# A PSUM bank lent to weight conversion, and the eighth attention unit in two-part operands

## The chip, the cores and the metric

The kernel runs on 1 core of one Trainium2 chip. The metric is the device time of one execution in microseconds. Before the change it is 1041.06 us, the median of 3 runs (1039.58 to 1042.63).

## The reference

Forget-gate attention, then two MLPs, all in float32 (the MLP weights arrive as float64):

```python
# q, k, v: 4 x 8 heads x 576 x 64; s: 4 x 8 x 576
cum = np.cumsum(np.maximum(s, 0.0), axis=-1)
scores = scale * q @ k^T + np.minimum(-(cum[..., :, None] - cum[..., None, :]), 0.0)   # causal
attn = np.exp(scores - rowmax); attn /= attn.sum(-1) + 1e-09
x = (attn @ v) as 2304 tokens x 512
r = np.maximum(x @ w_in, 0.0);  x = (s * (r * r) + b) @ w_out          # 512 -> 2048 -> 512
h = x @ w_in2;  out = (np.maximum(h, 0) + alpha * np.minimum(h, 0)) @ w_out2
```

## The kernel before

**Precision.** A product is made either with native float32 operands, which TensorE passes over twice (two records in the trace for one matmul), or with operands split into a high and a low fp32r part (`split`, L129): high x high, high x low, low x high. Attention's split form makes scores with two matmuls (L459, L460) where the native form has one (L457), and it splits the transposed probabilities into `ph` and `pl` instead of copying them to `pf` (L518 to L525).

**Attention.** A unit is one batch, one half of the tokens (`rng`: queries 0 to 319, or 320 to 575) and one pair of heads: 32 units. For each head, `scores` builds the bias in `probs` (VectorE L435, for the second head of a native unit ScalarE L431 with a sign flip), masks the diagonal on GpSimd (L439), adds TensorE's scores with a running extreme (L461), takes the exponential (L473), turns the sums round (L480, L481) and multiplies by them on GpSimd (L484). `values` transposes the probabilities (TensorE `pt`, L515), brings them to SBUF and multiplies by v (`av`, L531); the result goes into `xf`, the next layer's input. Units below `NATIVE` (L55, 8) use native float32, the others split operands. A split unit needs more: copies and differences of q and k (L393 to L401), the split of v into `vs` (L360 to L367), and the sum of two halves of `av` (L548, L549).

**Order.** Units 0 to 3 come first, with little beside them (0 to 61.6 us, "the head" here). Then layer 1 of the reference runs (called layer 0 in the code) in blocks of 256 tokens, `up` (L783) and `down` (L897) over 16 slices f of the 2048 hidden columns; units 4 to 7 are worked in beside block 0, the rest beside the later blocks. Block 1's input needs unit 7. The second MLP runs mostly in pairs of token blocks by Strassen's scheme: each pair of slices takes three banks a, b, c (L854), one of which (b) is read last by VectorE (L884). The instruction order on every engine is set by the framework's scheduler, which simulates a time line as it goes and gives pool buffers to whichever tile can have one; a change in any wait or buffer can reorder what follows.

**Weights.** Packet f holds slice f of both weight matrices. `fetch` loads 512 KB of raw pairs for each matrix on SyncE's queue, into whatever buffer the string `RAW` (L166) names: "raw", "xh1", "xl1", "xh0", "xl0", "res" or "vs". `convert` (L134) makes float32 of them in three steps over 128 x 512: ScalarE Prelu into `wt` (L140), VectorE shift of `wt` in place (L141), VectorE shift of the raw low word and OR with `wt` (L142); `split` then makes the high and low parts (L130 ScalarE, L131 VectorE for w_in and GpSimd for w_out). Packets 0 to 3 are asked for in the head, packets 4 to 15 during block 0, four slices ahead (`AHEAD`, L59).

**PSUM.** Eight banks of 128 x 512 float32: two for `acc0`, `acc1`, one for `hp`, one for `av`, and four with the tag "b", a pool from which scores, transposes and, in the later stages, `hp` and Strassen's a, b, c take any free one.

Of the kernel before, what the change touches and what calls it, by code (L numbers as in the profile page):

```python
# [8 lines left out]
F32 = mybir.dt.float32  # L9
F32R = mybir.dt.float32r  # L10
U32 = mybir.dt.uint32
BF16 = mybir.dt.bfloat16
AF = mybir.ActivationFunctionType
ALU = mybir.AluOpType
# [5 lines left out]
def tile_forget_attention__then__two_mlps(  # L20
# [20 lines left out]
    nc = tc.nc  # L41
    B, H, S, D = q.shape
    NT, DM = out.shape
    DFF = w_in1.shape[1] // 2
    P = 128
    NP = H // 2
    NCC = DM // P
    NF = DFF // P
    T = 256
# [2 lines left out]
    IB = [(0, 64)] + [(64 + 128 * n, 192 + 128 * n) for n in range(4)]  # L52
    R1 = IB[2][1]
    QK = S - R1 + S
    EARLY, NATIVE = NP, 2 * NP  # L55

    LAG, AHEAD, LEAD, PACE = (2, 3), 4, 4, 1.25  # L59
# [13 lines left out]
    ps = ctx.enter_context(tc.tile_pool(name="ps", bufs=2, space=PSUM))  # L73
# [24 lines left out]

    busy(16)

    def load_constants():
        nc.sync.dma_start(out=gate_s, in_=act_s.partition_broadcast(P))
        nc.sync.dma_start(out=gate_b, in_=act_b.partition_broadcast(P))
        nc.sync.dma_start(out=nalpha, in_=alpha.rearrange("(f p) -> p f", p=P))
        nc.vector.tensor_scalar(out=nalpha, in0=nalpha, scalar1=-1.0, scalar2=None, op0=ALU.mult)
        nc.vector.tensor_scalar(out=gate_s, in0=gate_s, scalar1=1.0 / W_SCALE, scalar2=None, op0=ALU.mult)
        nc.vector.tensor_scalar(out=gate_b, in0=gate_b, scalar1=1.0 / W_SCALE, scalar2=None, op0=ALU.mult)

    def sum_gates(first):

        nc.vector.tensor_scalar(out=gates, in0=gates, scalar1=0.0, scalar2=1.0 / SCALE, op0=ALU.max, op1=ALU.mult)
        ones = one.tile([B * H, S], F32, tag="vn", name="ones")
        nc.vector.memset(ones, 1.0)
        cum = two.tile([B * H, S], F32, tag="cum", name="cum")
        nc.vector.tensor_tensor_scan(out=cum, data0=ones, data1=gates, initial=0.0, op0=ALU.mult, op1=ALU.add)
        nc.scalar.dma_start(out=cum_d, in_=cum)
        for h, pool, tag in ((0, ps_h, "hp"), (1, ps, "av")):
            rows = pool.tile([P, 512], F32, tag=tag, name=f"rows{h}", bufs=1)[:, :R1]
            nc.tensor.matmul(
                rows, ident[: B * H, h : h + 1].to_broadcast([B * H, P]), cum[:, :R1], start=True, stop=True  # L120
            )
            first.cums.append(rows)
        tp = ps.tile([P, 5, B * H], F32, tag="b", bufs=4, name="tp")
        for r, (i0, i1) in enumerate(IB):
            nc.tensor.transpose(tp[: i1 - i0, r], cum[:, i0:i1], ident[: B * H, : B * H])
        nc.vector.tensor_copy(cumT[:64, 0], tp[:64, 0])
        nc.vector.tensor_copy(cumT[:, 1:], tp[:, 1:])
# [3 lines left out]
        lo_eng.tensor_tensor(out=lo, in0=src, in1=hi.bitcast(F32), op=ALU.subtract)  # L131


    def convert(raw, wt):  # L134

        low, high = raw[:, :, 0], raw[:, :, 1]

        nc.scalar.activation(wt.bitcast(F32), high.bitcast(F32), AF.Prelu, scale=REBASE, alpha=-(2.0**32))  # L140
        nc.vector.tensor_scalar(out=wt, in0=wt, scalar1=3, scalar2=None, op0=ALU.logical_shift_left)  # L141
        nc.vector.scalar_tensor_tensor(  # L142
            out=wt, in0=low, scalar=29, in1=wt, op0=ALU.logical_shift_right, op1=ALU.bitwise_or
        )

    def slot(n, dtype, name):
# [15 lines left out]
    PAIRS = {  # L162
        "r": [(two, "raw"), (two, "raw")], "x": [(one, "xh1"), (one, "xl1")], "y": [(one, "xh0"), (one, "xl0")],
        "v": [(one, "res"), (one, "vs")], "m": [(one, "res"), (two, "raw")], "n": [(two, "raw"), (one, "res")],
    }
    RAW = [pair for key in "rxyvrxvrxvrxvrmn" for pair in PAIRS[key]]  # L166
    SLOT, free = {}, list(range(NF))
    for f in range(len(SPARE), NF):
        at = int((f - len(SPARE)) * PACE)
# [46 lines left out]
    def load_packet(layer, f):  # L216
        wi, wo = fetch(layer, f)
        t = weight_tiles(f) if layer == 1 else []
        values_ = []
        for n, src in enumerate((wi, wo)):  # L220
            if layer == 1:
                pool, tag, cols = WT[(2 * f + n) % len(WT)]
                wt = pool.tile([P, cols], U32, tag=tag, name=f"wt{f}_{n}")[:, :512]
            elif (f, n) == (NF - 1, 1):
                wt = two.tile([P, 512], U32, tag="ph", name="last")
            else:
                wt = slot(WHOLE[f][n], U32, f"wt0_{f}_{n}")
            convert(src, wt)
            values_.append(wt.bitcast(F32))
        for n, wt in enumerate(values_):  # L230
            if layer == 0:
                t += [slot(m, F32R, f"w0_{f}_{len(t)}_{m}") for m in SPLIT[f][2 * n : 2 * n + 2]]
            split(t[2 * n], t[2 * n + 1], wt, nc.gpsimd if layer == 0 and n else nc.vector)
        return [x.rearrange("p (c n) -> p c n", c=NCC) for x in t[:2]] + t[2:]


    def sum_columns():

        ones = two.tile([P, T], F32, tag="r", name="ones")[:, :P]
        nc.gpsimd.memset(ones, 1.0)  # L240
        ones_r = two.tile([P, T], F32R, tag="r", name="ones_r")[:, :P]
        nc.scalar.copy(ones_r, ones)
        total = ps.tile([P, 512], F32, tag="b", name="colsum", bufs=4)
        for n in range(2 * NF):
            nc.tensor.matmul(total, ones_r, packet(0, n // 2)[2 + n % 2], start=(n == 0), stop=(n == 2 * NF - 1))
        colw = two.tile([P, 512], F32, tag="ph", name="colw")
        nc.scalar.copy(colw, total)
        turned = ps.tile([P, 512], F32, tag="b", name="colsum_t", bufs=4)
        for d in range(NCC):
            nc.tensor.transpose(turned[:, d * P : (d + 1) * P], colw[:, d * P : (d + 1) * P], ident)  # L250
        for d in range(NCC):
            nc.vector.tensor_scalar(
                out=bsum[:, d : d + 1], in0=turned[:, d * P : d * P + 1], scalar1=gate_b[:, 0:1], scalar2=None,
                op0=ALU.mult,
            )
# [22 lines left out]
    class Unit:  # L278
# [21 lines left out]
        def bank(self, tag, name):  # L300
            name = f"{name}_{self.tag}"
            self.n_banks += 1
            if self.n < EARLY and self.n_banks % 2:
                if tag == "tr":
                    return ps_h.tile([P, 512], F32, tag="hp", name=name)
                if tag == "av":
                    return acc_first
            if tag == "av":
                return ps.tile([P, 512], F32, tag="av", name=name, bufs=1)
            return ps.tile([P, 512], F32, tag="b", name=name, bufs=4)  # L310

    def qk_tiles(u, dtype, tag):

# [446 lines left out]
    def mlp_block(layer, t, x):  # L760
# [11 lines left out]
        def up(f):  # L772
            w = packet(layer, f)
            if layer == 0 and count == 1:
                hp = ps_h.tile([P, 512], F32, tag="hp", name=f"hp{layer}_{t}_{f}")
            else:
                hp = ps.tile([P, 512], F32, tag="b", name=f"hp{layer}_{t}_{f}", bufs=4)
            hs = hp[:, :TB]
            terms = ((w[0], xh), (w[0], xl), (w[1], xh))
            n = 0  # L780
# [65 lines left out]
        def up_first(f):  # L846

            name = f"{t}_{f}"
            (h1, l1), (h2, l2) = halves(f), halves(f + 1)
            left = {1: (h1[:, 0], l1[:, 0]), 2: (h1[:, 1], l1[:, 1]), 4: (h2[:, 1], l2[:, 1])}  # L850
            for n, k in ((5, 1), (6, 2), (7, 3), (3, 4)):
                both = sums[(k - 1) // 2][:, (k - 1) % 2]
                left[n] = both[:, : 2 * P], both[:, 2 * P :]
            a, b, c = (ps.tile([P, 512], F32, tag="b", name=f"p{z}_{name}", bufs=4)[:, :T] for z in range(3))  # L854
            t1, t5, u2 = temp("gh", f"t1_{name}", 3), temp("gl", f"t5_{name}", 3), temp("gh", f"u2_{name}", 3)
            multiply(a, 1, left[1], True)
            nc.scalar.copy(t1, a)
            multiply(b, 6, left[6], True)
            nc.vector.tensor_tensor(out=u2, in0=b, in1=t1, op=ALU.add)  # L859
            multiply(c, 5, left[5], True)  # L860
            nc.scalar.copy(t5, c)
            holder = []
            pair_state[f // 2] = left, (a, b, c), (t1, t5, u2), holder
            next_sums(f, (0, 1))
            return holder
# [121 lines left out]
    for n in range(len(BLOCKS) * NF):  # L987
        (layer, t), f = BLOCKS[n // NF], n % NF
        if f == 0:
            up, down, finish = mlp_block(layer, t, x)  # L990
            goal, x = reached(min(t + 1, NB - 1)) if layer == 0 else len(units), None
        late.append((down, finish, f, up(f)))
        if layer == 0 and t == 0 and f + AHEAD < NF:
            with tc.issue_after(relus[f - 1]) if f else nullcontext():
                packet(0, f + AHEAD)
            for g in range(f + AHEAD + 1, min(f + AHEAD + 3, NF)):
                fetch(0, g)
        if n == NF - 2:
            sum_columns()
        if len(late) > LAG[layer]:  # L1000
# [51 lines left out]
```

## Time and profile before

| What | Value |
|---|---|
| Time, median of 3 runs | 1041.06 us (1039.58 to 1042.63) |
| Profiled execution, whole | 1040.97 us |
| Its span (first to last work) | 1039.2 us |
| PE (TensorE matmul) busy | 1019.4 us, 98% |
| DVE (VectorE) / ACT (ScalarE) / POOL (GpSimd) busy | 66% / 65% / 44% |
| Granted TensorE clock, mean | 0.996 of full |

The page gives busy shares over the whole span. PE is the busiest by far, so time is gained where PE has less to do or waits less. The share does not tell at which places PE waits; those are read from stretches (windows) and time lines. In a time line the start of one matmul to the start of the next is what it costs, since matmuls are pipelined and their lengths overlap.

### The profile page before, as it was taken

What the parts mean: (1) busy time and instruction counts of PE and PEld (TensorE: products, weight loads), DVE (VectorE), ACT (ScalarE), POOL (GpSimd) and SP (SyncE); (2) the same over time, 40 slices, a digit from 0 to 9 for tenths busy, and PEclk for the clock granted to TensorE, in tenths of its full rate; (3) what the DMA queues carried; (4) which work ended last, traced back from release to release, by engine and by line L of the source; (5) the groups of instructions that cost most, each with busy time, mean ns of one, the idle gap of its engine ahead of it and who ended that gap; (6) DMA issues with size and microseconds to landing.
All of it is one profiled execution on the core that took longest, in us unless ns stands there. A gap on an engine that the chain in (4) does not pass through costs nothing. (4 is left out here: it accounts for less than half of the span.)

```text
span 1039.2 us, 20636 instructions
## 1 busy us (share of the span) xinstructions
PE 1019.4 (98%) x6952; PEld 925.8 (89%) x6952; DVE 681.3 (66%) x1605; ACT 672.4 (65%) x1669; POOL 457.6 (44%) x876
## 2 busy tenths in 40 slices
PE   9899999999999999999999999999999999999997
PEld 4568899999999999999999888888899999999996
DVE  6979865787676776677655865857665456455443
ACT  5877876777787877778776776645454455445433
POOL 5656775666677666777562000574611011001000
PEclk9999999999999999999999999999999999999999
DMA  7988433343232432334215762645644335334331
GB/s 167 255 211 239 132 68 70 71 93 79 40 92 64 102 72 52 79 68 91 66 35 173 240 192 74 207 147 170 196 163 142 103 112 172 103 99 136 104 104 46
DMA packets 197930, 125.45 MB, mean 121 GB/s; under 512 B 138496, under 2 KB 167936, under 8 KB 197824
## 3 DMA queue, kind: packets, MB, share of 16 engines
q1 hardware_dynamic: 193744, 123.56, 42.8%
q8 instruction: 55, 0.90, 0.4%
q10 hardware_dynamic: 4080, 0.57, 0.3%
q14 instruction: 51, 0.42, 0.1%
HBM read 106.19 MB, written 17.90 MB: 119 GB/s over the span
## 5 line engine op out<-in xcount | busy, mean ns | idle before, releaser
L783 PE MATMUL hp<-xh,w 128*128 128x256 f32 (+1 forms) x1024 | 229.0, 300 | 0.3 <-ACT r L802 0.3
L907 PE MATMUL acc<-w,ring 128*128 128x512 f32 x864 | 214.6, 392 | 1.1 <-DVE ring L131 0.7
L907 PEld LDWEIGHTS acc<-w,ring 128*128 128x128 f32 x864 | 155.8, 188 | 29.3 <-DVE ring L131 1.1
L783 PEld LDWEIGHTS hp<-xh,w 128*128 128x128 f32 x1024 | 171.4, 189 | 6.2 <-ACT r L802 0.5
L897 PE MATMUL acc<-gh,w 128*128 128x256 f32 x896 | 172.4, 286 | 0.5 <-ACT res L926 0.5
L783 PE MATMUL hp<-xl,w 128*128 128x256 f32 (+1 forms) x512 | 152.6, 298 | 0.0
L897 PEld LDWEIGHTS acc<-gh,w 128*128 128x128 f32 x896 | 136.0, 189 | 3.2 <-issue 1.6
L883 POOL TENSOR_TENSOR cc<-u,t 128x256 f32<-128x256 f32 x32 | 26.1, 817 | 235.5 <-DVE u L874 201.5
L897 PE MATMUL acc<-gl,w 128*128 128x256 f32 x448 | 118.7, 288 | 2.2 <-POOL gl L131 2.2
L484 POOL TENSOR_SCALAR probs<-probs,sm 64x64 f32<-64x64 f32 (+4 forms) x160 | 91.0, 581 | 60.5 <-DVE sm L481 49.9
L473 ACT ACTIVATE probs<-probs,nm 64x64 f32<-64x64 f32 (+4 forms) x160 | 90.0, 563 | 38.5 <-DVE nm L461 32.7
L131 POOL TENSOR_TENSOR gl<-r,gh 128x256 fp32r<-128x256 f32 x112 | 89.5, 799 | 48.6 <-ACT gh L130 42.1
L817 PE MATMUL p<-xs,sums 128*128 128x256 f32 x768 | 104.7, 282 | 0.4 <-DVE u L859 0.4
L783 PEld LDWEIGHTS hp<-xl,w 128*128 128x128 f32 x512 | 97.1, 190 | 3.3 <-issue 0.4
L817 PEld LDWEIGHTS p<-xs,sums 128*128 128x128 f32 x768 | 98.0, 189 | 2.1 <-DVE u L859 0.6
L461 DVE CUSTOM_DVE_ANT_0 probs<-sc,probs 128x320 f32<-128x320 f32 (+3 forms) x160 | 68.2, 427 | 41.2 <-PE sc L460 32.8
L817 PEld LDWEIGHTS p<-xs,w 128*128 128x128 f32 x576 | 79.0, 189 | 8.7 <-DVE u L874 2.0
L802 ACT ACTIVATE r<-hp 128x256 f32<-128x256 f32 (+1 forms) x144 | 58.0, 403 | 44.1 <-PE hp L783 33.2
L817 PE MATMUL p<-xs,w 128*128 128x256 f32 x576 | 82.3, 282 | 2.4 <-DVE u L874 1.5
L897 PEld LDWEIGHTS acc<-gl,w 128*128 128x128 f32 x448 | 80.1, 188 | 5.0 <-POOL gl L131 2.8
L828 DVE SCALAR_TENSOR_TENSOR ph<-pl,misc,ph 128x512 f32<-128x512 f32 x64 | 51.7, 807 | 42.4 <-ACT pl L844 42.4
L515 PE MATMUL pt<-ident,probs 128*128 128x128 f32 x480 | 74.3, 275 | 4.6 <-POOL probs L484 4.4
(149 smaller groups left out, 2116.8 us busy)
## 6 DMA issues: line engine op xcount, KB each, us to landing
sums<-sums_d SPq DMA_DIRECT2D x128, 256.0 KB, 2.7
wi<-in_moe_w_in_dram SPq DMA_DIRECT2D x32, 512.0 KB, 4.7
wo<-in_moe_w_out_dram SPq DMA_DIRECT2D x32, 512.0 KB, 4.8
cum<-cum_d SPq DMA_DIRECT2D x32, 288.0 KB, 3.7
sums_d<-w SPq DMA_DIRECT2D x64, 128.0 KB, 1.8
cum<-cum_d SPq DMA_DIRECT2D x30, 160.0 KB, 3.0
nat<-in_k_dram SPq DMA_DIRECT2D x64, 72.0 KB, 2.5
x_d<-res SPq DMA_DIRECT2D x18, 256.0 KB, 2.2
```

What stands on the lines that cost most here:

```text
L131: lo_eng.tensor_tensor(out=lo, in0=src, in1=hi.bitcast(F32), op=ALU.subtract)
L461: nc.vector.tensor_tensor_reduce(out=pt[:rows, j0:j1], in0=scr, in1=pt[:rows, j0:j1], scale=SCALE if flip else -SCALE, scalar=init, op0=AL ...
L473: nc.scalar.activation(pt[:rows, :n], pt[:rows, :n], AF.Exp, bias=nm[:rows, m : m + 1], scale=1.0 if flip else -1.0, accum_out=sm[:rows, m ...
L484: nc.gpsimd.tensor_scalar(out=probs[r][:rows, :n], in0=probs[r][:rows, :n], scalar1=sm[:rows, m : m + 1], scalar2=1.0, op0=ALU.mult, op1=A ...
L515: nc.tensor.transpose(tp[:, o : o + P], u.probs[h][r][:, k0 : k0 + P], ident)
L783: nc.tensor.matmul(hs, a[:, c], b[c], start=(n == 0), stop=(n == len(terms) * NCC - 1))
L802: relus.append(nc.scalar.activation(r, hs, AF.Relu, scale=1.0 / W_SCALE).ins)
L817: nc.tensor.matmul(bank, lhs[:, c * P : (c + 1) * P], rhs[:, c], start=(start and c == 0 and z == 0), stop=(c == 1 and z == 2), skip_group ...
L828: nc.vector.scalar_tensor_tensor(out=r, in0=u, scalar=nalpha[:, f : f + 1], in1=r, op0=ALU.mult, op1=ALU.add).ins
L883: nc.gpsimd.tensor_tensor(out=cc[:, T:], in0=u3, in1=t5, op=ALU.add)
L897: nc.tensor.matmul(banks[d] if count == 2 else acc[d // 2][:, d % 2], a[:, d * P : (d + 1) * P], b, start=(f == 0 and (d % 2 == 0 or count ...
L907: nc.tensor.matmul(banks[m], a[:, m * P : (m + 1) * P], b, start=(f == 0 and b is woh and a is gh), stop=(f == NF - 1 and a is gl),)
```

## The change

Four things change:

- `NATIVE` goes from 8 to 7: unit 7 (batch 0, second half, head pair 3), worked in beside the end of block 0, uses split operands.
- The tag "b" with four buffers becomes four tags b0 to b3 with one buffer each, handed out in a fixed rotation in the order in which the program asks (`bank`).
- From the first `up` of block 0 until slice 12, the rotation runs over three banks, and the fourth takes the result of the shift in `convert`: 24 conversions (packets 4 to 15, both matrices) shift from SBUF into PSUM, and OR from PSUM and the raw word into `wt`.
- In `RAW`, packet 12's w_out goes to "raw" where it had "vs", because unit 7 now has `vs`.

```diff
-    EARLY, NATIVE = NP, 2 * NP
+    EARLY, NATIVE = NP, 7
...
+    turn, lent = [0], []
+    def bank(name, n=None):
+        if n is None:
+            turn[0] += 1
+            n = turn[0] % (3 if lent else 4)
+        return ps.tile([P, 512], F32, tag=f"b{n}", name=name, bufs=1)
...
-    def convert(raw, wt):
+    def convert(raw, wt, shifted):
...
-        nc.vector.tensor_scalar(out=wt, in0=wt, scalar1=3, scalar2=None, op0=ALU.logical_shift_left)
+        nc.vector.tensor_scalar(out=shifted, in0=wt, scalar1=3, scalar2=None, op0=ALU.logical_shift_left)
         nc.vector.scalar_tensor_tensor(
-            out=wt, in0=low, scalar=29, in1=wt, op0=ALU.logical_shift_right, op1=ALU.bitwise_or
+            out=wt, in0=low, scalar=29, in1=shifted, op0=ALU.logical_shift_right, op1=ALU.bitwise_or
         )
...
-    RAW = [pair for key in "rxyvrxvrxvrxvrmn" for pair in PAIRS[key]]
+    RAW = [pair for key in "rxyvrxvrxvrxmrmn" for pair in PAIRS[key]]
...
-            convert(src, wt)
+            convert(src, wt, bank(f"bits{f}_{n}", 3).bitcast(U32) if lent else wt)
...
-            return ps.tile([P, 512], F32, tag="b", name=name, bufs=4)
+            return bank(name)
...
-            a, b, c = (ps.tile([P, 512], F32, tag="b", name=f"p{z}_{name}", bufs=4)[:, :T] for z in range(3))
+            a, b, c = (bank(f"p{z}_{name}")[:, :T] for z in range(3))
...
+        if n == 0:
+            lent.append(3)
...
+        if n == NF - AHEAD:
+            lent.clear()
```

The scheduler's order changes from the head onward. Two places, with the lines of each kernel's own file (L141, L142, L131, L375, L435, L480, L481 of before are L147, L148, L140, L381, L441, L486, L487 of after).

VectorE in the head, around the end of unit 3's second head (`sm_3_0_1` holds its sums; `wt_4` is packet 4, `turned_0_1` and `probs_0_1_0` belong to unit 4). Before:

```order
L470 TENSOR_SCALAR nm_3_0_1_722<-nm_3_0_1_722 128x1
L141 TENSOR_SCALAR wt_4_0_901<-wt_4_0_901 128x512
L131 TENSOR_TENSOR xl_0_870<-xf_433,xh_0_869 128x256
L142 SCALAR_TENSOR_TENSOR wt_4_0_901<-wi_4_272,wt_4_0_901 128x512
L375 STREAM_TRANSPOSE turned_0_1_695<-nat_0_1_564 128x832
L131 TENSOR_TENSOR w_3_0_11_654<-wt_3_0_645,w_3_0_12_653 128x512
L435 TENSOR_SCALAR probs_0_1_0_817<-cum_0_0_1_573,cumT 128x448
L435 TENSOR_SCALAR probs_0_1_0_817<-cum_0_0_1_573,cumT 128x576
L141 TENSOR_SCALAR wt_4_1_905<-wt_4_1_905 128x512
L480 TENSOR_SCALAR sm_3_0_1_723<-sm_3_0_1_723 128x3
L142 SCALAR_TENSOR_TENSOR wt_4_1_905<-wo_4_273,wt_4_1_905 128x512
L481 RECIPROCAL sm_3_0_1_723<-sm_3_0_1_723 128x3
```

The same place after:

```order
L147 TENSOR_SCALAR wt_3_1_649<-wt_3_1_649 128x512
L148 SCALAR_TENSOR_TENSOR wt_3_1_649<-wo_3_263,wt_3_1_649 128x512
L381 STREAM_TRANSPOSE turned_0_1_695<-nat_0_1_564 128x832
L140 TENSOR_TENSOR xl_0_870<-xf_433,xh_0_869 128x256
L486 TENSOR_SCALAR sm_3_0_1_723<-sm_3_0_1_723 128x3
L441 TENSOR_SCALAR probs_0_1_0_817<-cum_0_0_1_573,cumT 128x448
L441 TENSOR_SCALAR probs_0_1_0_817<-cum_0_0_1_573,cumT 128x576
L487 RECIPROCAL sm_3_0_1_723<-sm_3_0_1_723 128x3
L140 TENSOR_TENSOR w_3_0_11_654<-wt_3_0_645,w_3_0_12_653 128x512
```

Packet 4's four instructions are no longer ahead of unit 3's last RECIPROCAL; they come later.

TensorE at the end of unit 7 (`av_0_3_1`; `acc_0` and `hp_0` are block 0, `hp_1_0` is block 1's first slice, `sc` the scores of unit 8). Before, where `hp_1_0` begins some fifty matmuls further on:

```order
L897 MATMUL acc_0_0_879<-gl_0_12_2014,w_12_2_50_1672 128x256
L897 MATMUL acc_0_1_880<-gh_0_12_2013,w_12_2_50_1672 128x256
L897 MATMUL acc_0_1_880<-gh_0_12_2013,w_12_2_49_1673 128x256
L897 MATMUL acc_0_1_880<-gl_0_12_2014,w_12_2_50_1672 128x256
L531 MATMUL av_0_3_1_1790<-pf_3_1_1_0_1796,vn_3_1_1475 128x256 x2
L897 MATMUL acc_0_1_880<-gh_0_12_2013,w_12_2_50_1672 128x256
L531 MATMUL av_0_3_1_1790<-pf_3_1_1_1_1811,vn_3_1_1475 128x256
L531 MATMUL av_0_3_1_1790<-pf_3_1_1_1_1811,vn_3_1_1475 128x192
L531 MATMUL av_0_3_1_1790<-pf_3_1_1_1_1811,vn_3_1_1475 128x64
L897 MATMUL acc_0_1_880<-gh_0_12_2013,w_12_2_49_1673 128x256
L897 MATMUL acc_0_1_880<-gl_0_12_2014,w_12_2_50_1672 128x256
L897 MATMUL acc_0_0_879<-gh_0_13_2210,w_13_2_54_1884 128x256
```

After, where nine of the twelve matmuls of `hp_1_0` have been issued already (the row is the tenth, which needs unit 7):

```order
L537 MATMUL av_0_3_1_1841<-ph_3_1_1_1_1866,vs_all 128x192
L537 MATMUL av_0_3_1_1841<-ph_3_1_1_1_1866,vs_all 128x64
L537 MATMUL av_0_3_1_1841<-pl_3_1_1_1_1867,vs_all 128x256
L537 MATMUL av_0_3_1_1841<-pl_3_1_1_1_1867,vs_all 128x192
L537 MATMUL av_0_3_1_1841<-pl_3_1_1_1_1867,vs_all 128x64
L465 MATMUL sc_0_0_1_0_0_2115<-xs_1_0_0_1759 128x64
L466 MATMUL sc_0_0_1_0_0_2115<-xs_1_0_0_1759,ql_114 128x64
L465 MATMUL sc_2_0_1_0_0_2152<-xs_1_0_0_1759 128x320
L466 MATMUL sc_2_0_1_0_0_2152<-xs_1_0_0_1759,ql_114 128x320
L465 MATMUL sc_1_0_1_0_0_2135<-xs_1_0_0_1759 128x192
L466 MATMUL sc_1_0_1_0_0_2135<-xs_1_0_0_1759,ql_114 128x192
L789 MATMUL hp_1_0_2406<-xh_1_1899,w_0_0_0_204 128x256
```

Unit 7's values moved from beside block 0's `down` over slices 12 and 13 to just ahead of block 1's tenth matmul, with six matmuls of unit 8 between.

## Rows read from the trace of the kernel before

**Rows 1.** three windows: busy us (instructions) per engine, granted clock, DMA share, GB/s

```profile
61.60:148.07 86.47, 85.27 (x582) 74.02 (x580) 72.89 (x158) 69.05 (x169) 59.29 (x92) 1.00 0.64 164
545.00:660.00 115.00, 115.00 (x594) 97.84 (x593) 78.72 (x135) 80.97 (x155) 12.41 (x13) 1.00 0.56 176
660.00:1039.00 379.00, 369.71 (x2311) 332.77 (x2309) 207.65 (x359) 178.71 (x421) 85.62 (x99) 1.00 0.41 131
```

**Rows 2.** timeline of PE, the head: start, length, work [idle before <-releaser]

```profile
53.76 0.55 PE L515 MATMUL pt<-ident,probs 128*128 128x128 f32 x3 [2.79 <-POOL probs L484]
```

**Rows 3.** timeline of POOL, the head

```profile
50.88 1.70 POOL L439 TENSOR_SCALAR_AFFINE_SELECT probs<-probs 128x128 f32<-128x128 f32 x3
52.69 1.52 POOL L484 TENSOR_SCALAR probs<-probs,sm 64x64 f32<-64x64 f32 x3
```

**Rows 4.** timeline of DVE, the head

```profile
51.16 0.51 DVE L141 TENSOR_SCALAR wt<-wt 128x512 uint32<-128x512 uint32 x1
...
51.76 0.68 DVE L142 SCALAR_TENSOR_TENSOR wt<-wo,wt 128x512 uint32<-128x512 uint32 x1
52.36 0.16 DVE L481 RECIPROCAL sm<-sm 128x3 f32<-128x3 f32 x1
```

**Rows 5.** timeline of PE, 115 to 124: native attention units

```profile
115.33 1.23 PE L457 MATMUL sc<-turned 64*128 64x320 f32 x4
116.50 1.09 PE L515 MATMUL pt<-ident,probs 128*128 128x128 f32 x8
...
120.01 1.02 PE L457 MATMUL sc<-turned 64*128 64x448 f32 x2
120.96 0.51 PE L897 MATMUL acc<-gh,w 128*128 128x256 f32 x2
...
121.42 1.95 PE L531 MATMUL av<-pf,vn 128*128 128x256 f32 x10
123.18 0.72 PE L897 MATMUL acc<-gh,w 128*128 128x256 f32 x4
```

**Rows 6.** timeline of PE, 210 to 250: units in two parts

```profile
210.78 0.39 PE L459 MATMUL sc<-xs 128*128 128x320 f32 x1
...
211.15 0.28 PE L459 MATMUL sc<-xs 128*128 128x256 f32 x1
...
211.39 0.38 PE L515 MATMUL pt<-ident,probs 128*128 128x128 f32 x2
...
244.56 0.40 PE L531 MATMUL av<-ph,vs_all 128*128 128x256 f32 x2
...
245.63 0.33 PE L515 MATMUL pt<-ident,probs 128*128 128x128 f32 x1
...
248.99 0.37 PE L459 MATMUL sc<-xs 128*128 128x448 f32 x1
...
249.40 0.28 PE L897 MATMUL acc<-gl,w 128*128 128x256 f32 x1
```

**Rows 7.** groups of DVE by form, block 0 (count, busy us, mean ns)

```profile
L141 DVE TENSOR_SCALAR wt<-wt 128x512 uint32<-128x512 uint32 x21 | 14.4, 691 | 2.8 <-ACT wt L140 2.6
L142 DVE SCALAR_TENSOR_TENSOR wt<-wi,wt 128x512 uint32<-128x512 uint32 x11 | 11.7, 1060 | 0.2
...
L142 DVE SCALAR_TENSOR_TENSOR wt<-wo,wt 128x512 uint32<-128x512 uint32 x10 | 8.0, 795 | 0.1
L519 DVE COPY pf<-pt 128x512 f32<-128x512 f32 x8 | 5.4, 676 | 0.9 <-PE pt L515 0.9
```

**Rows 8.** groups of DVE by form, 545 to 660

```profile
L141 DVE TENSOR_SCALAR wt<-wt 128x512 uint32<-128x512 uint32 x31 | 14.7, 478 | 7.2 <-ACT wt L140 6.6
```

**Rows 9.** page, part 6: DMA issues, KB each, median us to landing

```profile
wo<-in_moe_w_out_dram SPq DMA_DIRECT2D x32, 512.0 KB, 4.8
```

**Rows 10.** timeline of PE, 141.9 to 148.3: end of block 0

```profile
142.29 0.36 PE L897 MATMUL acc<-gh,w 128*128 128x256 f32 x1
...
148.07 0.28 PE L783 MATMUL hp<-xh,w 128*128 128x256 f32 x1
```

More of the change, by code (lines that the diff above doesn't have):

```diff
@@ L122, in sum_gates @@
             first.cums.append(rows)
-        tp = ps.tile([P, 5, B * H], F32, tag="b", bufs=4, name="tp")
+        tp = bank("tp")[:, : 5 * B * H].rearrange("p (r h) -> p r h", h=B * H)
         for r, (i0, i1) in enumerate(IB):
@@ L242, in sum_columns @@
         nc.scalar.copy(ones_r, ones)
-        total = ps.tile([P, 512], F32, tag="b", name="colsum", bufs=4)
+        total = bank("colsum")
         for n in range(2 * NF):
@@ L247, in sum_columns @@
         nc.scalar.copy(colw, total)
-        turned = ps.tile([P, 512], F32, tag="b", name="colsum_t", bufs=4)
+        turned = bank("colsum_t")
         for d in range(NCC):
@@ L776, in up @@
             else:
-                hp = ps.tile([P, 512], F32, tag="b", name=f"hp{layer}_{t}_{f}", bufs=4)
+                hp = bank(f"hp{layer}_{t}_{f}")
             hs = hp[:, :TB]
```

## The prediction

> **What bounds the kernel now.** I read the windows first. In block 0 PE is busy 85.27 of 86.47 us and DVE 72.89, POOL 59.29; over the Strassen part PE is busy 369.71 of 379 [rows 1]. So PE sets the pace almost everywhere, and an edit is worth what it takes from PE's work, from its 1.20 us of idle time in block 0, from its 9.3 us in the last part, or from the head. In the head the time line of PE shows one wait that is large: 2.79 us ahead of 53.76, for the GpSimd multiplication L484 [rows 2]. Behind that stands a queue: POOL starts L484 at 52.69, just after an affine select that ends at 52.58 [rows 3]; the RECIPROCAL it needs ran on DVE at 52.36, with a shift and an OR of packet 4 around it [rows 4]. The time lines of the attention units give what native and split operands cost [rows 5, 6], and the groups of DVE what the conversions cost beside a busy POOL and beside a quiet one [rows 1, 7, 8].
>
> **Unit 7 in two parts: the surest term.** Native, one head of a second-half unit takes on PE, from start to start: 320 and 256 columns of scores 116.50 - 115.33 = 1.17 us, 448 columns 120.96 - 120.01 = 0.95, values 123.18 - 121.42 = 1.76 [rows 5]; together 3.88. In two parts: 320 columns 211.15 - 210.78 = 0.37, 256 columns 211.39 - 211.15 = 0.24, 448 columns 249.40 - 248.99 = 0.41, values 245.63 - 244.56 = 1.07 [rows 6]; together 2.09. Two heads save 2 x 1.79 = 3.6 us. The transposes stay. This is PE's own work in a stretch where PE is busy 99% [rows 1], so all of it comes off unless a wait fills it. Bounds: 3.6 saved to nothing.
>
> Its cover is DVE, which gets more to do. I take 1.32 ns a column from the 0.676 us of a 512-column copy from PSUM [rows 7]: four low parts of probabilities less two copies 1.35, two differences of k over 576 columns 1.52, two of q over 256 0.68, the sums of `av` halves over 192 and 64 columns 0.68, the second head's bias (576 and 448 columns) on DVE instead of ACT 1.35: 5.6 us more, hidden so long as DVE is not late.
>
> **The shift into PSUM.** In block 0 a conversion costs DVE 0.691 for the shift and, over both matrices, (11.7 + 8.0) / 21 = 0.94 for the OR, 1.63 together [rows 7]. Where POOL is busy only 12.41 of 115 us the same shift takes 0.478 [rows 1, 8]. So some of block 0's price is time in which the two engines hold each other up. Afterwards neither instruction has two operands in SBUF. No row has a shift into PSUM; the nearest is the copy from PSUM, 0.676, and I take 0.68 for each of the two: 1.36. 24 x 0.27 = 6.5 us less DVE work. From both sides: if the relief is full on the OR and the shift stays at 0.478, 24 x 0.47 = 11 less; if the relief doesn't come at all, the shift costs 0.2 more than the quiet one on top of what it costs now, 24 x 0.2 = 5 more. With unit 7's 5.6 DVE is about where it was, near 72 of then 83 us, and POOL is held up less. I count -0.8 us of PE's 1.20 us of idle time, bounds -1.2 to +3. The one lent bank makes each shift wait for the OR before it; both are on DVE, whose queue is in order, so that is no wait of another engine.
>
> The Trainium skill, page "SBUF — State Buffer", section "Who interferes with whom", says that a VectorE instruction with two SBUF inputs, or in a two-port mode, and a GpSimd one that reads SBUF exclude each other for a whole instruction; the trace agrees, 0.691 against 0.478 for one shift. By that page the loan works. Its page "VectorE: DVE Perf Modes", section "Why PSUM operands drop a tier", speaks against it: a float32 operand in PSUM loses the fast mode. In rows 0.676 against 0.478 is in line with that. What it would do here is a rival below.
>
> **The head.** Packet 4's shifts and ORs no longer stand ahead of unit 3's last RECIPROCAL. Of those, 0.51 + 0.68 is in sight right before it, and the other pair was ahead of them [rows 4]: some 2.4 us of DVE work. PE's wait can shrink by 2.79 at most [rows 2]. POOL is the second in line: its selects ended at 52.58 [rows 3] and themselves wait for DVE's bias, which moves forward too. I take -2.0, bounds 0 (POOL is late anyway) to -2.8. What moves behind, packet 4's conversion, is needed four slices later.
>
> **The junction of blocks 0 and 1.** Before, unit 7's values end at 142.29 and block 1 begins at 148.07 [rows 10]; its tenth matmul, which needs unit 7, is nine of 0.12 us later, so about 6.9 us lie between. After, only six matmuls of unit 8's scores do (about 0.8 us), and the chain is a copy of 192 columns on ACT, a sum on DVE, and a rounding copy of 256 columns: at 1.32 ns a column 0.25 + 0.25 + 0.34, with three hand-overs and whatever is queued before them. The values ahead of it wait in turn for the low part on DVE, 0.68. I take +2.0 of new waiting; bounds 0 to +5.
>
> **The fixed rotation.** Four named banks instead of any free one can only bind more: a tile waits for its own bank though another is free. In block 0 three serve scores and transposes; in the last part a Strassen pair's a, b, c take three of four, so the next pair's third matmul group must wait for the last reader of the previous b, on DVE. PE's idle time there is 9.3 us for 32 pairs [rows 1]. I take +0.3, bounds -1 (another order by chance) to the rival below.
>
> **The later load.** Packet 13's w_out now loads after packet 12's conversion has emptied "raw": one landing, 4.8 us [rows 9], in series. A slice of block 0 is 86.47 / 16 = 5.4 us and packets are asked for four slices ahead, so I count 0; without the cover it is up to 4.8. The other moved DMAs stay in their order on SyncE.
>
> **Sum.** -3.6 - 0.8 - 2.0 + 2.0 + 0.3 = -4.1. The span goes from 1039.2 to 1035.1; with the 1.77 us around it the profiled execution goes from 1040.97 to 1036.9. The median of the runs is 0.09 above the profiled execution: 1037.0.
>
> **Rivals.**
> - More comes off: the head gives 2.8, block 0 1.2, the junction waits 0.3 only: -3.6 - 1.2 - 2.8 + 0.3 = -7.3, about 1033.8. For it: the wait of 2.79 is real and single. Against: the order puts unit 7 right ahead of its user.
> - The junction eats the gain: DVE is late by the 5.6 us that unit 7 adds, the chain behind unit 7 costs 5, and block 0 gets 0.7 more idle time: -3.6 - 2.0 + 0.7 + 5 + 0.3 = +0.4, about 1041.4. For it: DVE's 84% in block 0 [rows 1]. Against: in the time line block 0 has only 1.20 us of PE waiting with nearly the same load.
> - The loan doesn't do what it says: the shift into PSUM takes 0.68 and POOL holds DVE up as before. Then DVE has 72.9 + 5.6 + 5 = 83.5 us to do in 82.9, and it bounds block 0; with the 1.2 us of idle time that PE keeps and 2 us for its uneven load: -3.6 - 2.0 + 0.6 + 2 + 2 = -1.0, about 1040. This is where the page on PSUM operands would lead. For it: 0.676 against 0.478. Against: 1.63 us for a conversion now.
> - Slower: the fixed rotation binds in the Strassen part. Each of the 32 pairs starts its third group after two groups of six matmuls (12 x 0.12 = 1.4 us); if the last reader of b (256 columns, 0.34) comes a full instruction later than that, 32 x 0.34 = 10.9: -4.1 - 0.3 + 10.9 = +6.5, about 1047.5. It decides from some 0.25 us a pair on. For it: all four tags are single. Against: between the last reader and that third group lies also the `down` of another slice, and PE's 9.3 us of idle time leaves 0.29 a pair now.
>
> **How the numbers follow.** What a measurement can tell from no change is 0.3%, 3.1 us: faster is below 1037.9, slower above 1044.2. Forecast 0.48, own range 1034.5 to 1039.5 (0.40 of it faster, 0.08 the same); more comes off 0.13, faster; junction 0.15, the same; loan without effect 0.07, the same; rotation 0.17 (0.15 slower, 0.02 the same). Faster 0.53, same 0.32, slower 0.15. The range of 8 in 10 takes the forecast's, the low rival down to 1032.5 and the two middle ones up to 1043.
>
> **What would show it.** Unit 7: PE's matmuls of L457 fewer by 12 records and the scores and values of unit 7 at the lengths of [rows 6]. Loan: block 0's shift near 0.68 and OR near 0.68 without tails. Head: PE's wait for L484 below 1 us, and block 0's first `up` about 2 us sooner. Junction: an idle time of some 2 us ahead of the tenth matmul of block 1. Rotation: idle time over 660 to the end within 1 us of 9.3. The forecast is wrong if the junction's wait is over 5 us, or if the last part grows by more than 3.

## The result: slower, 1051.5 us

The changed kernel takes 1051.53 us (median, 1050.13 to 1052.42) against 1040.91 for the kernel before: a ratio of 1.0099, interval 1.0086 to 1.0113, 10.6 us. Forecast were 1037.0, a range of 1032.5 to 1043.0, and 0.15 for slower. Of the runs used below, one of e7 (1113.89 us, granted clock 0.847) is left out as slow, and five of the 19 of the kernel before beside e1 to e4 took 1047.1 to 1047.9 us at a granted clock of 0.988, which makes those four intervals wide.

The first view is again that of the windows: before and after over the same two stretches and over the whole way from block 0's first matmul to the first of the Strassen part, and after over block 0 and the Strassen part (busy us of PE, PEld, DVE, ACT, POOL, then granted clock, DMA share, GB/s). Before:

```profile
139.00:155.00 16.00, 16.00 (x132) 15.82 (x131) 9.63 (x35) 11.79 (x35) 13.78 (x32) 1.00 0.32 68
155.00:550.00 395.00, 392.41 (x3238) 388.79 (x3236) 271.13 (x783) 302.09 (x804) 260.43 (x548) 1.00 0.32 73
61.67:689.84 628.17, 623.30 (x4601) 587.97 (x4600) 448.33 (x1129) 468.84 (x1179) 358.29 (x689) 1.00 0.41 107
```

After:

```profile
61.80:139.00 77.20, 76.55 (x534) 67.49 (x534) 64.84 (x143) 63.30 (x153) 46.61 (x75) 1.00 0.71 180
139.00:155.00 16.00, 11.87 (x67) 10.94 (x67) 11.24 (x35) 10.79 (x29) 10.26 (x25) 0.68 0.27 57
155.00:550.00 395.00, 388.79 (x3178) 382.92 (x3177) 276.46 (x796) 298.03 (x798) 261.03 (x555) 1.00 0.33 73
671.00:1050.00 379.00, 369.90 (x2308) 332.56 (x2306) 203.48 (x358) 178.54 (x421) 83.47 (x99) 1.00 0.43 131
61.80:700.47 638.67, 626.59 (x4597) 590.54 (x4597) 449.24 (x1142) 468.95 (x1182) 352.94 (x692) 0.99 0.41 106
```

From 139 to 155 us PE makes 67 matmuls where it made 132. It is idle for 4.1 us, and its granted clock is 0.68 on average. What the clock costs is counted on PE's busy time alone: by the narrow windows at the end of this document, 0.05 x 3.32 + 0.50 x 3.31 + 0.47 x 4.24 = 3.8 us. Together that is some 7.9 us, an estimate; the 65 missing matmuls at 16.00 / 132 = 0.12 us each give the same. From 155 to 550 PE is idle for 3.6 us more, and in block 0 for 0.65 instead of 1.20 us [rows 1]. The Strassen part is unchanged, 369.90 of 379 [rows 1].

Over the whole way from block 0 to the Strassen part, 10.5 us longer, PE is idle for 12.08 us where it was idle for 4.87, 7.2 more, and the clock takes 3.8. Its busy time less those 3.8 is 622.8 us where it was 623.3: only 0.5 less, though unit 7 needs 3.6 less. Where the other 3 us of busy time arose is not shown. The first Strassen matmul comes at 700.47 where it came at 689.84, 10.6 us later.

**The junction.** The time line of PE in the changed kernel, from block 1's first matmul on:

```profile
139.03 0.30 PE L789 MATMUL hp<-xh,w 128*128 128x256 f32 x1
...
140.12 0.40 PE L537 MATMUL av<-ph,vs_all 128*128 128x256 f32 x2
...
141.19 0.33 PE L521 MATMUL pt<-ident,probs 128*128 128x128 f32 x1
141.88 1.09 PE L521 MATMUL pt<-ident,probs 128*128 128x128 f32 x8 [0.36 <-POOL probs L490]
144.29 0.45 PE L465 MATMUL sc<-xs 128*128 128x320 f32 x1 [1.32 <-DVE xf L555]
...
146.16 0.83 PE L537 MATMUL av<-pl,vs_all 128*128 128x256 f32 x3
...
147.84 0.63 PE L465 MATMUL sc<-xs 128*128 128x320 f32 x1 [0.43 <-DVE nm L467]
148.27 0.47 PE L466 MATMUL sc<-xs,ql 128*128 128x320 f32 x1
150.76 0.53 PE L465 MATMUL sc<-xs 128*128 128x192 f32 x1 [2.02 <-DVE last L148]
151.08 0.42 PE L466 MATMUL sc<-xs,ql 128*128 128x192 f32 x1
151.30 0.47 PE L789 MATMUL hp<-xh,w 128*128 128x256 f32 x1
```

and what it waits for on DVE, and on ACT:

```profile
140.22 0.33 DVE L467 CUSTOM_DVE_ANT_0 probs<-sc,probs 128x192 f32<-128x192 f32 x1
...
143.47 0.68 DVE L140 TENSOR_TENSOR pl<-pt,ph 128x512 fp32r<-128x512 f32 x1
...
149.42 0.36 DVE L555 TENSOR_TENSOR xf<-av,xf 64x192 f32<-64x192 f32 x1
...
150.02 0.69 DVE L148 SCALAR_TENSOR_TENSOR last<-wo,bits 128x512 uint32<-128x512 uint32 x1
```

```profile
147.89 0.31 ACT L554 COPY xf<-av 64x192 f32<-64x192 f32 x1
...
150.33 0.41 ACT L139 CAST xh<-xf 128x256 fp32r<-128x256 f32 x1
```

Block 1 begins 9 us sooner than before (148.07, [rows 10]); its tenth matmul comes at 151.30, and from 143 to 151 PE mostly stands behind scores of unit 8. By the order in which `bank` hands out numbers, the 320 columns at 144.29 have bank 1, which unit 7's transposes hold until the low part at 143.47 has read them (it ends at 144.15; the row names L555, which follows it on DVE); the 192 columns at 150.76 have bank 3, the lent one, which the last packet's OR at 150.02 still reads. Block 1's tenth matmul stands behind both in PE's order. By the same count bank 2 was free beside both waits: its last scores were read at 140.22, and its next tile is written at 151.57.

The bank is not all that the tenth matmul needed. It reads `xh`, which the cast on ACT at 150.33 makes, done at 150.74. From the end of unit 7's last values (146.16 + 0.83 = 146.99) the chain of copy, sum and cast took 3.75 us to there, though its three instructions are 0.31, 0.36 and 0.41 us long; between them stood work of unit 8 and of the last packet on both engines. Without the last score's wait the tenth could have begun only some 0.5 us sooner.

**The head.** Block 0's first `up` starts at 61.80, before at 61.67. The wait of 2.79 us for unit 3's L484 [rows 2] is gone, but unit 4's scores, moved ahead of it, now wait, and an earlier wait for that line (L490 here) is 1.60 us:

```profile
43.29 0.55 PE L521 MATMUL pt<-ident,probs 128*128 128x128 f32 x3 [1.60 <-POOL probs L490]
...
48.34 3.78 PE L463 MATMUL sc<-turned 64*128 64x448 f32 x6 [3.84 <-DVE turned L381]
```

```profile
47.24 1.04 DVE L381 STREAM_TRANSPOSE turned<-nat 128x832 f32<-128x832 f32 x1 [0.98 <-DMA nat<-in_k_dram]
```

DVE had time for the transpose, and then waited 0.98 us for unit 4's k from memory. The 3.78 us of the six scores are at a granted clock of 0.50; before, at 1.00, the same six took

```profile
49.01 1.96 PE L457 MATMUL sc<-turned 64*128 64x448 f32 x6 [0.57 <-DVE turned L375]
```

**The loan.** DVE's groups in block 0, after:

```profile
L147 DVE TENSOR_SCALAR bits<-wt 128x512 uint32<-128x512 uint32 x21 | 14.5, 689 | 3.0 <-ACT wt L146 2.7
L148 DVE SCALAR_TENSOR_TENSOR wt<-wi,bits 128x512 uint32<-128x512 uint32 x11 | 7.5, 683 | 0.1
L148 DVE SCALAR_TENSOR_TENSOR wt<-wo,bits 128x512 uint32<-128x512 uint32 x10 | 6.8, 684 | 0.1
```

The OR fell from 1060 and 795 ns to 684, the shift stayed at 0.69 [rows 7]: 1.37 us a conversion where 1.36 was forecast.

### The profile page after: what moved, and what is told of

Read it like the earlier page. It is cut to its first block, busy times and chain, and to the rows that moved or that the text cites. A ratio compares the mean times of both kernels' runs of the same rounds, so it can differ in the third digit from the quotient of the medians.

```text
span 1050.6 us, 20738 instructions
## 1 busy us (share of the span) xinstructions
PE 1022.4 (97%) x6952; PEld 928.7 (88%) x6952; DVE 675.8 (64%) x1615; ACT 672.4 (64%) x1673; POOL 452.2 (43%) x879
## 5 line engine op out<-in xcount | busy, mean ns | idle before, releaser
L140 POOL TENSOR_TENSOR gl<-r,gh 128x256 fp32r<-128x256 f32 x112 | 86.9, 777 | 69.3 <-ACT gh L139 44.6
L490 POOL TENSOR_SCALAR probs<-probs,sm 64x64 f32<-64x64 f32 (+4 forms) x160 | 96.2, 614 | 40.3 <-DVE sm L487 26.9
L823 PE MATMUL p<-xs,sums 128*128 128x256 f32 x768 | 108.0, 282 | 0.4 <-DVE u L865 0.4
L823 PEld LDWEIGHTS p<-xs,sums 128*128 128x128 f32 x768 | 100.3, 189 | 2.7 <-DVE u L865 0.6
L823 PE MATMUL p<-xs,w 128*128 128x256 f32 x576 | 84.7, 282 | 2.3 <-DVE u L880 1.5
L521 PE MATMUL pt<-ident,probs 128*128 128x128 f32 x480 | 77.8, 277 | 4.1 <-POOL probs L490 4.1
L884 DVE TENSOR_TENSOR u<-p,u 128x256 f32<-128x256 f32 x32 | 13.6, 424 | 89.8 <-PE p L823 89.8
```

The lines of the kernel that those rows point to most:

```text
L490: nc.gpsimd.tensor_scalar(out=probs[r][:rows, :n], in0=probs[r][:rows, :n], scalar1=sm[:rows, m : m + 1], scalar2=1.0, op0=ALU.mult, op1=A ...
L521: nc.tensor.transpose(tp[:, o : o + P], u.probs[h][r][:, k0 : k0 + P], ident)
L823: nc.tensor.matmul(bank, lhs[:, c * P : (c + 1) * P], rhs[:, c], start=(start and c == 0 and z == 0), stop=(c == 1 and z == 2), skip_group ...
L884: nc.vector.tensor_tensor(out=u2, in0=c, in1=u2, op=ALU.add)
```

## The experiments

All are set against runs of the kernel before on the same chip (medians 1040.6 to 1041.3). "Loss" below is PE's idle time from 120 to 165 us plus 45 us times what the granted clock lacks to 1. It is an upper figure, since idle time at the lower clock counts twice. Before has none, the changed kernel 4.55 + 0.11 x 45 = 9.5.

**One part at a time.** e1 has the naming alone; e2 adds the loan (`NATIVE` and `RAW` as before); e3 is the changed kernel without the loan; e4 is the kernel before with

```diff
-    EARLY, NATIVE = NP, 2 * NP
+    EARLY, NATIVE = NP, 7
-    RAW = ... "rxyvrxvrxvrxvrmn"
+    RAW = ... "rxyvrxvrxvrxmrmn"
```

and e5 has the second of these lines alone.

> Only the four banks are named b0 to b3 and handed out in rotation; nothing is lent, units 0 to 7 stay native, RAW as before. In the changed kernel's trace PE loses 8.3 us more than before between 140 and 160 us, and some 6 us more in small waits from 160 to 550 us. Theory A (unit 7 comes too late for block 1, PE runs dry and its clock falls to half): in this order unit 7's last values stand 184 matmuls ahead of block 1's tenth instead of 7, so nothing is lost there and the time is 1038 to 1044. Rival B (the fixed rotation itself costs, everywhere): 1046 to 1052, with small waits spread over 160 to 550 us.

> Named banks and the lent bank for 24 conversions, but unit 7 stays native. Unit 7's last values stand 17 matmuls ahead of block 1's tenth. Theory A: most of the junction's loss is there without the split of unit 7, since the lent bank leaves attention three banks and lets the MLP run ahead: 1047 to 1053, granted clock at half for some us near 140 to 160. Rival C (the longer chain of the split unit 7 is what makes it late): the junction costs under 2 us, 1040 to 1045. Rival B: as named banks alone, within 2 us.

> Named banks and unit 7 in two parts with the changed RAW, but nothing lent: conversions shift in place. Unit 7's last values stand 52 matmuls ahead of block 1's tenth. Theory A: no junction loss, unit 7 saves 3.6: 3 to 4 us under names alone. Rival C: a junction loss of 5 to 8 us as in the changed kernel. Rival B: names alone less 3.6, so 1042 to 1048.

> The kernel before with nothing but unit 7 in two parts and the changed RAW; four banks from the pool as before, nothing lent. Unit 7's last values stand 15 matmuls ahead of block 1's tenth. If unit 7's 3.6 us come off and the 15 matmuls hide the chain: 1037 to 1038.5. Theory A with the distance in matmuls as what decides: some junction loss, 1039 to 1044. Rival C: 1044 to 1049.

> The kernel before with one buffer changed: packet 12's w_out is loaded into "raw" and no longer into "vs"; units, banks and conversions as before. Names alone, and the split alone, each cost some 8 us, and all of the variants lose it in PE waits between 110 and 165 us, each behind another instruction. Theory D (the order of before at the end of block 0 is a lucky or tuned one, and whatever makes the scheduler lay it out anew loses there): 1044 to 1050, with waits of PE in 110 to 165 us. Rival E (each part has a cost of its own, and this one only moves a load by one landing): 1040 to 1043.

| | us | ratio, interval | loss 120 to 165 |
|---|---|---|---|
| e1 names | 1048.35 | 1.0071, 1.0045 to 1.0097 | 5.8 |
| e2 names, loan | 1055.17 | 1.0133, 1.0095 to 1.0171 | 5.3 |
| e3 names, split | 1051.29 | 1.0091, 1.0052 to 1.0129 | 10.6 |
| e4 split, pool | 1049.34 | 1.0069, 1.0041 to 1.0097 | 11.6 |
| e5 RAW only | 1043.49 | 1.0031, 1.0017 to 1.0044 | 1.2 |
| changed | 1051.53 | 1.0099, 1.0086 to 1.0113 | 9.5 |

Every part alone makes the kernel slower, and they don't add up. By time only e1 fell in a range that was given, rival B's; e5 came between its two, e4 just above rival C's, e2 and e3 outside of all times given (e3 with 5.5 us of loss from 140 to 160, as rival C had it). The naming costs 7.3 us though 184 matmuls lie between unit 7 and block 1's tenth; theory A, which counted that distance, falls with it. The loss sits in 120 to 150 us, not over 160 to 550 as rival B had it (the window from 155 to 550 has PE at 392.82, before 392.41). The split costs 8.3 on the pool too (by the interval 4 to 10), and e5 tells that some 3 of them come with the later load. From e2 to the changed kernel, where unit 7 is split, the median falls by 3.6 us. That this is what its matmuls were priced at is chance: the intervals overlap, and the two lose in different places (PE from 155 to 550: 385.01 and 388.79). The waits of e1 and of e4 (time line of PE), each behind another instruction:

```profile
127.81 0.33 PE L521 MATMUL pt<-ident,probs 128*128 128x128 f32 x1 [1.70 <-POOL probs L490]
...
133.55 2.06 PE L537 MATMUL av<-pf,vn 128*128 128x256 f32 x10 [0.78 <-ACT pf L525]
...
144.40 0.50 PE L537 MATMUL av<-ph,vs_all 128*128 128x320 f32 x2 [0.71 <-POOL vs_all L140]
```

```profile
136.95 1.07 PE L897 MATMUL acc<-gh,w 128*128 128x256 f32 x4 [1.64 <-ACT gh L130]
...
157.33 0.47 PE L531 MATMUL av<-ph,vs_all 128*128 128x320 f32 x2 [1.42 <-POOL probs L426]
...
160.64 0.30 PE L531 MATMUL av<-pl,vs_all 128*128 128x64 f32 x1 [1.29 <-DVE pl L131]
```

These waits are for probabilities and parts that GpSimd, ACT or DVE makes, not for a bank: how the naming alone costs 7.3 us, beyond the new order, stays open.

**Single waits of the junction taken away.** e6 keeps packet 15 out of the loan (`if lent and f < NF - 1`); e9 puts the last conversion into another buffer, and e10 does the same to the kernel before:

```diff
-                wt = two.tile([P, 512], U32, tag="ph", name="last")
+                wt = two.tile([P, 1024], U32, tag="raw", name="last")[:, :512]
```

e11 is the changed kernel with `LEAD` 5 for 4, e12 has both.

> The changed kernel, but packet 15's two conversions shift in place, not into the lent bank. In the changed kernel's trace the longest wait at the junction, 2.02 us at 150.76, is unit 8's score matmul waiting for the OR of that last conversion, which reads the lent bank that the score takes next. Theory F (the loan's return is a cause): that wait goes and with it part of the half clock, 1045 to 1049. Theory D: other waits come in its place, 1050 to 1054.

> The changed kernel, but the buffer of the last conversion (packet 15's w_out) is "raw" and not "ph", which attention's transposed probabilities use. In the trace of the changed kernel that packet's raw words landed at 128.6 us, but its Prelu ran at 145.7 and its OR at 150.0, behind unit 7's parts in "ph"; before it was 125.8, 138.8 and 141.4. Theory H (block 0's last down and the column sums, 24 and 32 matmuls that could fill PE at 140 to 152, wait for that packet): the conversion is done by 140, the loss of 9.3 us from 140 to 160 falls to 3 to 5, the time to 1045 to 1048. Rival (unit 7's own chain is what block 1 waits for): loss and time within 1.5 us of the changed kernel's 1051.5.

> The kernel before with the same one move, the last conversion's buffer in "raw". The order hardly changes: unit 7's last values stand 66 matmuls ahead of block 1's tenth, 58 before. Theory H: nothing waited for it before, so 1040 to 1043. Theory D (any new layout loses at the end of block 0): 1043 to 1048.

> The changed kernel with LEAD 5 for 4: attention is asked for a quarter of a slice sooner each slice; unit 7's values end 43 matmuls ahead of block 1's tenth, not 7. If unit 7's lateness is what costs: the loss of 9.3 us from 140 to 160 falls by 4 or more, 1045 to 1048. If the last conversion is what costs (theory H): within 1.5 us of 1051.5.

> The changed kernel with LEAD 5 and the last conversion's buffer in "raw". If the two waits stand side by side at the junction, so that taking one away uncovers the other, only this one helps: junction loss under 4 us, 1043 to 1046. If one of them alone is the cause: as the better one of the two single edits.

e6 took 1046.96 (1.0065, 1.0044 to 1.0087), as theory F had it, but not where it had it: the 2.02 us are gone, and PE waits for others there, with a loss of 10.5:

```profile
143.31 0.39 PE L465 MATMUL sc<-xs 128*128 128x320 f32 x1 [1.32 <-DVE xf L555]
146.42 0.64 PE L465 MATMUL sc<-xs 128*128 128x320 f32 x1 [1.08 <-DVE nm L467]
148.81 0.80 PE L903 MATMUL acc<-gh,w 128*128 128x256 f32 x2 [1.49 <-ACT w L139]
```

e9 took 1053.26 (1.0106, 1.0070 to 1.0142). The last conversion was done by 133 us, 18 sooner, and PE is still idle for 4.28 us from 120 to 165. Its loss is 8.3 as counted above, but some 2 of these come from a granted clock that this one profile puts at 0.95 over the whole execution, with a time like that of its other three runs (0.991 to 0.992). So the loss fell to some 6, and the time did not fall with it: theory H falls. e10 took 1040.64 (0.9996, 0.9978 to 1.0014): this move costs nothing, so not any change of layout loses. e11 took 1056.14 (1.0156, 1.0101 to 1.0211), e12 1056.41 (1.0142, 1.0102 to 1.0182): no gain, and the medians are above the changed kernel's, though the intervals still touch. In e11 the loss from 140 to 160 falls from 9.4 to 5.3, as its first theory had it, and the time doesn't follow: PE is at 385.87 from 155 to 550. In e12 the loss from 120 to 165 is only 1.6, but PE is at 381.45 from 155 to 550, 11 below before. The waits move; they don't go.

**The order forced back.** e13 to e15 hold the `up` of block 0's last slices behind unit 7 (e14 as below; e13 from slice 15, e15 from 13 and behind the transposes):

```diff
+                    tails[u.n, h] = nc.tensor.matmul(...).ins    # in values()
...
+        with tc.issue_after(tails[7, 1]) if layer == 0 and t == 0 and f >= 14 else nullcontext():
             late.append((down, finish, f, up(f)))
```

> The changed kernel; the up of block 0's slice 15 is issued only behind unit 7's last value matmul, so that this slice's up and down stay as filler. Unit 7's values end 28 matmuls ahead of block 1's tenth. Theory J: the loss of 9.3 us from 140 to 160 falls by 3 to 5, 1046 to 1049. If the chain itself is what costs, whatever stands beside it: no gain, 1050 to 1054.

> As e13 with slices 14 and 15 held: unit 7's values end 60 matmuls ahead of block 1's tenth, as before the change (58). Theory J: loss from 140 to 160 under 4 us, 1044 to 1047. Otherwise 1050 to 1054.

> Slices 13 to 15 held behind unit 7's last transposes: 75 matmuls between. Theory J: as e14 or 1 us better, 1043 to 1047; PE may wait sooner, for unit 7's probabilities, if attention is bound by the other engines: then the loss moves to 115 to 140 us and the time is 1047 to 1052.

They took 1054.25 (1.0131, 1.0113 to 1.0148), 1048.13 (1.0083, 1.0056 to 1.0110) and 1049.55 (1.0087, 1.0064 to 1.0109). e13 is just above its second range and e14 between its two; only e15's second branch came as given, with 6.9 us of loss from 115 to 140. Theory J falls: with the distance of before, e14's loss from 140 to 160 is 4.0, but from 120 to 165 it is 10.5, only sooner:

```profile
134.88 0.33 PE L465 MATMUL sc<-xs 128*128 128x192 f32 x1 [1.94 <-DVE pl L140]
136.73 0.51 PE L539 MATMUL av<-ph,vs_all 128*128 128x256 f32 x2 [1.41 <-POOL vs_all L140]
139.97 0.48 PE L523 MATMUL pt<-ident,probs 128*128 128x128 f32 x1 [1.50 <-POOL probs L490]
```

Where e14's median is below the changed kernel's (the intervals overlap), the gain lies from 155 to 550: PE is at 392.93 there again.

**The loan with a pool.** e7 (loan alone) and e8 (with the split) take the shift's target from the kernel before's pool of four. e16 is the changed kernel with a pool of three and one named bank, e17 is e16 with unit 7 native and the old `RAW`, e18 is e16 with the edits of e6 and e9:

```diff
-            n = turn[0] % (3 if lent else 4)
-        return ps.tile([P, 512], F32, tag=f"b{n}", name=name, bufs=1)
+            n = 0 if lent else turn[0] % 4
+        tag, bufs = ("c", 1) if n == 3 else ("b", 3)
+        return ps.tile([P, 512], F32, tag=tag, name=name, bufs=bufs)
```

> The kernel before, units and RAW as before; the 24 conversions shift into a PSUM buffer taken from the pool of four, not into a bank of their own. Theory D: a new order, a loss in 110 to 165 us, 1044 to 1050. Rival G (the loan helps as long as banks are not named): shift and OR near 0.69 us each, VectorE's contention goes, 1037 to 1041.

> As the changed kernel, but with the pool of any four free banks in place of the named ones: shifts into PSUM buffers from the pool, unit 7 in two parts, changed RAW. Unit 7's last values stand 90 matmuls ahead of block 1's tenth. Rival G: unit 7's 3.6 us come off on top, 1034 to 1038. Theory D: 1042 to 1050. Rival B (naming is what costs): 1037 to 1041.

> The changed kernel, but three banks are a pool of any free one, and the lent bank alone has a name; outside the loan every fourth tile takes it. If naming costs by itself (names alone cost 7.3 us): 1043 to 1047. If the loan and the order do: 1049 to 1054.

> As e16, but unit 7 native and RAW as before: the loan alone, beside a pool of three. If unit 7's split chain is what is left of the cost: PE runs through the end of block 0 (77 matmuls between unit 7's values and block 1's tenth) and the time is 1038 to 1042. If the loan costs by itself (three banks for attention): 1044 to 1050.

> As e16, but packet 15's two conversions shift in place and the last one's buffer is "raw": the 1.03 us that PE waits there for the last OR, and the 0.38 behind it, go. 33 matmuls between unit 7's values and block 1's tenth, where e16 has 5. If these waits are what is left: 1040 to 1043, level with the kernel before or under it; if the chain of unit 7 is: 1044 to 1047.

e7 took 1058.19 (1.0152, 1.0108 to 1.0196), e8 1058.80 (1.0168, 1.0144 to 1.0192): outside every theory. Their longest waits in block 0 are of `up`, for the ReLU on ACT (2.9 and 3.1 us) and for weights from DVE (1.7 and 2.0); I did not follow them further. e16 took 1045.35 (1.0049, 1.0030 to 1.0068), in the range given for naming: 6 us of the 10.6 go with the naming of the three other banks, and the loss is 4.4 at a full clock. e17 took 1044.81 (1.0044, 1.0028 to 1.0060), with no loss worth naming at the junction (PE 44.45 of 45 at full clock), and e18 1044.69 (1.0038, 1.0022 to 1.0055). e17 fell in the range of "the loan costs by itself": with unit 7 native the kernel is still 3.5 us slower, so the split chain is not needed for most of what is left in e16. Its waits lie from 155 to 550 (idle 5.84 us, before 2.59), where the loan is over but every fourth tile still takes the one named bank; which of the two costs them is not shown. e18 fell in the range given for unit 7's chain, but e17, without that chain, takes the same. None is faster than the kernel before.

## Why the prediction was wrong

- **Unit 7's matmuls**, -3.6: right as PE's work. L463 has 12 records fewer than L457 had, and one head's values take 141.19 - 140.12 = 1.07 us in the changed kernel, the price of [rows 6]. e4 differs from e5 in unit 7 alone; from block 0's first matmul to the Strassen part PE is busy 624.22 us there, 3.2 of them lost to the lower clock, against 624.78 in e5: 3.8 less. As time it didn't come off. What was not priced is the rest of the step: its longer chain through GpSimd's split of v and DVE's low parts, and the later load. e4 against before is +8.3 with the 3.6 in it, so some 12 gross, an estimate from medians.
- **The loan**: right as a mechanism and in size on DVE (1.37 for 1.36), but not shown as a gain in block 0: from 62 to 120 us PE is idle for 0.28 us where it was for 1.20, and in e1, which has no loan, not at all. The Trainium skill, page "SBUF — State Buffer", section "Who interferes with whom", says that a VectorE instruction with at most one SBUF input, outside the two-port modes, does not contend with GpSimd; the trace agrees for the OR, 1060 and 795 ns with two SBUF inputs and 684 with one. As time the loan paid in no pair that differs in it: e1 to e2 +6.8 us, e3 to the changed kernel +0.2, before to e17 (with its one named bank) +3.5, before to e7 some 16.
- **The head**, -2.0: wrong. I followed the queue of one wait and not what stood next on PE. Unit 4's scores wait for a load that lands at 47 us; freed DVE time cannot move that.
- **The junction**, +2.0 with bounds 0 to +5: the step that failed; it measured some 7.9, 4.1 of waits and 3.8 of the lower clock. The mechanism (unit 7 right ahead of its user) was named, but the sum put the chain at the 0.84 us of its three instructions, with the queues ahead of them left without a number; it took 3.75. Missing were also unit 8's scores, in PE's order between, with banks that unit 7 and the last packet still hold, and any term for the clock, which after the first waits stayed low for ten us. The waits alone lay inside the bounds; with the clock's 3.8 the term left them.
- **The rest of the attention**, not in the sum: PE's idle time from 155 to 550 grew by 3.6.
- **The fixed rotation**, +0.3: wrong in size and place. It was priced as a rival for the Strassen part, where nothing changed (369.90 of 379). Its cost came at the end of block 0, where attention hands its banks over: +7.3 alone (e1), 6 of the changed kernel's 10.6 (e16). These are largely the same microseconds as the junction's, not further ones.
- **The later load**, 0: e5 shows +2.9 (ratio 1.0031), inside the bound of 4.8: the term was wrong to be nothing.

So the slower side came in part by the rival's cause, in another place; the split without any naming (e4) costs as much. What stays open is how much of each part's cost is a real lack (banks, GpSimd, a landing) and how much the order that the scheduler then chose: e6, e9 and e11 to e15 moved the loss without taking it away, and e10, which leaves the order nearly alone, costs nothing. That the order of before happens to fit the chip there is argued, not shown.

## What to carry to other kernels

When a scheduler sets the order, an edit is worth what the new order makes of it: price the terms of the edit, then read PE's new order at the stage's end and ask, for each instruction ahead of the one that matters, which buffer it needs and who holds it, and when its input can be ready with the work that is queued ahead of it. A buffer with a fixed name can make a matmul wait while another bank is free, as here at 144.29 and 150.76, and everything behind it in PE's order waits too. And a busy engine's saving (for DVE some 6 us here, 24 x 0.26) is worth only what the bounding engine was waiting for it.

## What the runs showed of the hardware

The granted clock of PE after short waits. In the changed kernel PE was idle for 0.37 us ahead of 138.75 and for 0.36 and 1.32 us from 141.5 to 144.3, and the windows then show the lower level, 1.2 of 2.4 GHz, for most of ten us:

```profile
140.00:145.00 5.00, 3.32 (x25) 2.92 (x24) 2.83 (x11) 2.25 (x6) 3.60 (x12) 0.95 0.44 82
145.00:150.00 5.00, 3.31 (x15) 2.78 (x13) 3.50 (x13) 3.70 (x10) 1.46 (x2) 0.50 0.33 76
150.00:155.00 5.00, 4.24 (x21) 4.24 (x22) 3.91 (x11) 4.15 (x12) 4.28 (x10) 0.53 0.11 23
```

The further waits of 0.43 and 2.02 us lie in this stretch. What the stretch costs beside the waits is what PE's busy time in it lacks, 3.8 us as worked out above. e16, with waits of 1.03, 0.38, 0.16 and 0.27 us from 144 to 148, kept the full clock (1.00 from 139 to 155, PE busy 13.53 of 16 us).
